# Windowed attention and a GELU feed-forward on one core: batch 1's denominators by pairs of pairs, its value products late, batch 0's tail queries loaded earlier

## Chip, cores and metric

The kernel runs on one core of a Trainium2 chip. The metric is the device time of one execution in microseconds (us). The core has five engines with instruction queues of their own: TensorE (PE; its weight loads are listed as PEld), VectorE (DVE), ScalarE (ACT), GpSimd (POOL) and SyncE (SP, which here only issues transfers). Each engine works through its queue in order. In the profile "PEq", "SPq" and so on are the sequencers; L613 is line 613 of the kernel.

## What is computed

```
# q, k, v: (8 batches, 8 heads, 576 positions, 64); w_in: (512, 2048); w_out: (2048, 512); float32
scores = (q @ k^T) / 8,  allowed where |i - j| <= 32
attn   = softmax(scores) @ v
x      = attn as (8 * 576 tokens, 512)
h      = x @ w_in
out    = (0.5 * h * (1 + tanh(c * (h + 0.044715 h^3)))) @ w_out        # 4608 x 512, float32
```

## The kernel before

**Tiles and stages.** The 4608 tokens go through the feed-forward in nine tiles of 512 (`t` = 0 to 8); a batch has 576 tokens. Attention is worked on by batch and, in it, by pairs of heads: four groups `g` = 0 to 3 of a pair each, for the first 480 positions (512 in batch 0), and a fifth group, the tail, for the last 96 (64) positions of all pairs. A stage `t` has two parts: products with `w_in` and GELU (`ffn_in`, 64 matmuls of 512 columns), then products with `w_out`. The second part of stage `t` is a loop over steps `i`, one output matmul each (`ffn_out_0`: 64 of 512 columns in stage 0; `ffn_out`: 112 of 256 columns from stage 1 on, a seven-product scheme `WINO` over halves of the matrices whose sums and differences DVE forms, L548 and L558). Between the steps batch `t + 1`'s attention is interleaved, and the tail of batch `t`. So stage 0's loop holds batch 1's attention and batch 0's tail, stage 1's loop holds batch 2's and batch 1's tail.

**The plan.** What comes before step `i` is written by hand in the dictionaries `PLAN_0` (stage 0), `PLAN_1` (stage 1) and `PLAN` (later): a letter, a group (-1 is the tail of the batch before), and after `@` which of two PSUM tiles (`S0`, `S1`, two banks each) is used.
- `s`: scores on PE and Exp on ACT (L410, L422). `m`: the mask, a DVE product with `band` (L428).
- `v`: `weigh` and `invert`: the sums (`ones` times the masked exps, L433), the products with values (L443), then the reciprocal of the sums on ACT as exp(-ln(sum)): L468 Ln, L469 Exp. Without `@` its two banks are `O` and `D`.
- `x`: `spread`, the DVE product of value products and reciprocals into `xT` (L478; L484 for a tail). It frees the banks.
- Stage 0 alone: `r` casts and transposes a pair of batch 1's queries and keys (L282 casts, L310 and L312 transposes, L317 and L318 copies out); `t` transposes batch 0's tail queries (L299, copied out by DVE in L303); `w`, `u` cast a quarter of `w_out` (L213) on DVE, POOL and ACT; `d` is `pair_chunk`, the DVE copies (L193, L195) that put a chunk of batch 1's V beside the next one; `c` starts the sums of `w_out` (L548).

The bank of a tile is taken again only when what was in it has been read: `v2@1` of stage 0 waits for `x0`, since both use `S1`.

**Transfers.** SP issues the loads of weights, queries and keys in program order. `tails_0` loads batch 0's last 64 queries (L154) and keys (L156) into a tile `tr`; `tails` loads batch 1's into the same buffer, so that SP waits there until `cast_tails` (L294) has read batch 0's. In the kernel before POOL does that cast of the queries at step 26, with `w2`. Then SP issues the last quarter of `w_out` (`wo[3]`) and, with `u3`, batch 2's queries and keys (`load_qk`, L168 to L173). Batch 1's V is loaded by POOL (`load_v`, L178, casting on the way; `load_vt`, L182). Batch 2's q and k are cast by DVE after stage 0 (L338, L362) and transposed by DMA (L341, L364); behind these SP loads batch 2's V (L370), which POOL casts (`cast_v`, L289) and DVE pairs (`pair_v`, L187 and L188) at steps 17 and 40 of stage 1, four heads each (`PAIR_1`). At step 4 of a stage POOL waits for the last key transpose (`after`, L819) and loads the next batch's V.

**DVE, stage 1.** The output products' seven results are taken out of PSUM by DVE when their 16 steps are done: M1 after step 15 (L624), U2 after 31 (L626), C11 after 47 (L628), U3 after 63 (L633), C22 after 79 (L636), C21 after 95 (L642).

Of the kernel before, what the change touches and what calls it, by code (L numbers as in the profile page):

```python
# [9 lines left out]
FP32 = mybir.dt.float32  # L10
# [26 lines left out]
def cut(b):  # L37
# [11 lines left out]

PLAN_0 = {8: "r2@0", 10: "s0@1", 11: "w1", 14: "s1@0", 19: "r3@1", 22: "m0 s2@0", 25: "s3@1", 26: "m1 w2",
          30: "t-1@0 m2", 35: "s-1@0 m3", 38: "d0", 39: "m-1", 40: "d1", 43: "v-1@0", 44: "d2 x-1 d3", 46: "w3",
          48: "v0@1 v1@0", 50: "x0 x1", 54: "v2@1", 55: "u3", 58: "v3@0 x2", 59: "x3", 60: "c1"}
PLAN_1 = PLAN | {10: "s0@0", 12: "s1@1", 18: "m0 m1", 33: "s2@0", 40: "v0@1 v1", 50: "x0", 53: "x1", 62: "s3@0 v2",
                 64: "s-1@1", 66: "m3", 70: "m-1", 76: "x2", 78: "v-1@1", 84: "x-1", 88: "s4@1", 91: "v3", 98: "m4"}
for i in (4, 16, 44, 80):
    del PLAN_1[i]
PAIR_1 = {17: slice(0, 4), 40: slice(4, 8)}

# [9 lines left out]
def kernel(  # L70
# [129 lines left out]
    def stage_w():  # L200
        return stage.tile([128, 4, 512], FP32, name="wst", tag="stage")
# [394 lines left out]
    def ffn_out(t, i):  # L596

        n, blk, f = i // 16, i // 8 % 2, i % 8
        a, w, new = WINO[n]
        end = t == NT - 1  # L600
        if i % 16 == 0 and new:
            pys[n % 2] = bank((1 + n) % 2)
            if end and n == 4:
                pys["apart"] = psO.tile([128, 512], FP32, name="py2", tag="O")
        py = pys[n % 2].rearrange("p (b c) -> p b c", b=2)
        apart = end and blk and n in (4, 6)
        if a[0] == "A":
            r0, c0 = 8 * (int(a[2]) - 1) + f, 256 * (int(a[1]) - 1) + 128 * blk
            lhsT = gTs[t][:, r0, c0:c0 + 128]
        else:  # L610
            lhsT = wino[a][:, f, 128 * blk:128 * blk + 128]
        one = end and n in (4, 6)
        nc.tensor.matmul(pys["apart"][:, 0:256] if apart else py[:, blk, :], lhsT,  # L613
                         wino[w][:, f, :], start=(new and i % (8 if one else 16) == 0),
                         stop=(i % (8 if one else 16) == (7 if one else 15)),
                         skip_group_check=True)
        if i % 16 < 15:
            return
        yo, left, right = wino["yo"], slice(0, 256), slice(256, 512)
        C11, C12, C21, C22 = (yo[:, r:r + 2, c] for r in (0, 2) for c in (left, right))  # L620

        M1, U2, U3 = C21, C12, C22
        if n == 0:
            nc.vector.tensor_copy(M1, py)  # L624
        elif n == 1:
            nc.vector.tensor_tensor(U2, py, M1, op=ALU.add)  # L626
        elif n == 2:
            nc.vector.tensor_copy(C11, py)  # L628
            if end:
                for x in range(2):  # L630
                    store(t, x, yo[:, x, :], left, nc.sync)
        elif n == 3:
            nc.vector.tensor_tensor(U3, py, M1, op=ALU.add)  # L633
        elif n == 4:
            if not end:
                nc.vector.tensor_tensor(C22, py, U3, op=ALU.add)  # L636
            else:
                for x, part in enumerate((py[:, 0, :], pys["apart"][:, 0:256])):
                    nc.vector.tensor_tensor(C22[:, x, :], part, U3[:, x, :], op=ALU.add)
                    store(t, 2 + x, yo[:, 2 + x, :], right, nc.sync, nc.scalar)  # L640
        elif n == 5:
            nc.vector.tensor_tensor(C21, py, M1, op=ALU.add)  # L642
            for x in range(2):
                store(t, 2 + x, yo[:, 2 + x, :], *((left, nc.sync, nc.scalar) if end else ()))
# [98 lines left out]
    for n in range(4):  # L743
        ffn_in(0, n, 3, 4)
    cast_w(wi[2], w_in16[:, :, 1024:1536], (0, 2))
    wo.append(load_w_out(1, stage_w()))
    qk(6)
    wo.append(load_w_out(2, stage_w()))
    tails_0("q")
    tails()  # L750
    wo.append(load_w_out(3, stage_w(), 0, 2))
    load_w_out(3, wo[3], 2, 4)
# [24 lines left out]
    trans_pair(1, 1, psO.tile([128, 8, 128], FP16, name="pt", tag="O"))  # L777
    cast_early(1, 2, (nc.vector, nc.vector))
    load_v(1, (2, 3))

    def spare(i):
        pt = psS.tile([128, 2, 8, 128], FP16, name="pt", tag=f"S{i}")
        return pt[:, 0], pt[:, 1]


    begun = 0
    for t in range(NT):
        b = t + 1
        att = b < B
        if t:  # L790
            for fc in range(begun):
                ffn_in(t, fc, 3, 4, then=False)
            for fc in range(begun):
                gelu(t, fc)
            if att and b > 1:
                rest = cast_and_turn(b)
            for fc in range(begun, NF):
                ffn_in(t, fc)
                if t == 1 and fc in (3, 4, 5, 6):
                    cast_v(2, fc - 3)  # L800
                if t == 1 and 9 <= fc < 14:
                    rest(fc - 9)
                if t == 1 and fc == 8:
                    trans_tails(1, psO.tile([128, 8, 128], FP16, name="pt", tag="O"))
                if t > 1 and fc == 8 and att:
                    pair_v(b, nc.vector.tensor_copy)
        plan = PLAN_0 if not t else PLAN_1 if t == 1 else PLAN if att else {5: "v-1", 31: "x-1"} if t == B - 1 else {}

        def group(g):
            return (b, g) if g >= 0 else (b - 1, 4)  # L810

        if plan and t:
            load_table(exp_set)
        if t and b + 1 < B:
            load_qk(b + 1)
        ods = {}
        for i in range(113 if t else 65):
            if t and i == 4 and b + 1 < B:
                nc.gpsimd.tensor_copy(after, KLs[b % 2][:, 3, 0:1])  # L819
                load_v(b + 1)  # L820
            for act in plan.get(i, "").split():
                kind, at = act[0], int(act[act.index("@") + 1:]) if "@" in act else None
                g = int(act[1:].split("@")[0])
                if kind == "w":
                    if g == 3:
                        cast_w(wo[g], w_out16[:, 12:16, :], cs=(0, 1), on_dve=(0,))
                    else:
                        cast_w(wo[g], w_out16[:, 4 * g:4 * g + 4, :], on_act=(1, 3))
                    if g == 1:
                        load_vt(1)  # L830
                    if g == 2:
                        cast_tails(0, nc.gpsimd, even)
                elif kind == "t":
                    trans_tails(0, spare(at)[0], even)
                elif kind == "r":
                    if g == 3:
                        cast_early(1, 3, (nc.vector, nc.vector))
                    trans_pair(1, g, *spare(at), copy=nc.scalar.copy)
                elif kind == "u":
                    cast_w(wo[g], w_out16[:, 12:16, :], on_dve=(3,), cs=(2, 3))  # L840
                    cast_tails(1, nc.gpsimd)
                    load_qk(2)
                elif kind == "c":
                    if g == 1:
                        B12 = combine_w()
                    combine(g, nc.vector)
                elif kind == "s":
                    score(*group(g), at)
                elif kind == "d":
                    pair_chunk(b, g, nc.vector.tensor_copy)  # L850
                elif kind == "m":
                    mask(*group(g))
                elif kind == "v":
                    bb, gg = group(g)
                    o, d = weigh(bb, gg, at)
                    ods[g] = (o, invert(bb, gg, d))
                    if t and g < 0 and b + 1 < B:
                        load_vt(b + 1)
                    if t and g == (3 if att else -1):
                        load_table(gelu_set)  # L860
                else:
                    spread(*group(g), *ods[g])
            if t == 1 and i == 30:
                cast_vt(2)
            if t == 1 and i in PAIR_1:
                pair_v(2, nc.vector.tensor_copy, PAIR_1[i])
            if t == 0 and i in (61, 62):
                store(0, *later.pop(0), slice(0, 512), nc.scalar)
            if t == 0 and i < 64:
                ffn_out_0(*ORDER_0[i])  # L870
            elif t and i < 112:
                ffn_out(t, i)
        if t == 0:
            for t4, yo in later:
                store(0, t4, yo)
            wino_rest(B12)
            load_table(gelu_set)
        else:
            ffn_last(t)
        begun = 3 if t < NT - 1 else 0  # L880
        for fc in range(begun):
            ffn_in(t + 1, fc, 0, 3)
# [28 lines left out]
```

## Time and profile before

| | |
|---|---|
| median of 6 runs | 304.02 us (303.69 to 305.15) |
| profiled execution | 304.11 us, its span 302.4 us |
| granted TensorE clock, mean | 0.992 |
| PE busy | 289.1 us, 96% of the span |
| DVE busy | 194.1 us, 64% |
| ACT busy | 194.1 us, 64% |
| POOL busy | 92.3 us, 31% |

The span runs from the first to the last instruction of the program. All times in the text are counted from its start. A busy PE is one whose matmuls are in flight; holes in it are found by engine and cause in the view of waits ("who waited: by whom released: us in total, times, longest"). The chain is the run of work that ended last, followed backwards. Stage 0's output part runs from 36.7 to 58.3 us, stage 1's first part to 72.4 and its output part to 92.8; each later stage takes about 30.4 us.

### The profile page before, as it was taken

To read this page: it belongs to the slowest core of one execution; us is meant where nothing else is said; L and a number is where in the kernel's file an instruction comes from. 1 tells how busy PE (TensorE), PEld (TensorE's weight loads), DVE (VectorE), ACT (ScalarE), POOL (GpSimd) and SP (SyncE) were. 2 spreads that over 40 slices of the span, in tenths; PEclk is the share of its full clock that TensorE was granted. 3 is DMA by queue.
4 is the path that set the end of the run, shared out by engine and by line. 5 is a ranking of instruction groups with operands and counts; after the bars stand their busy time and mean duration, and the time that the engine had idled before them with its cause. 6 is when DMAs were issued, how large, how long until landed. Compare 5 with 4: busy or idle time off the path is not lost.

```text
span 302.4 us, 7116 instructions
## 1 busy us (share of the span) xinstructions
PE 289.1 (96%) x2898; PEld 180.3 (60%) x2898; DVE 194.1 (64%) x435; ACT 194.1 (64%) x306; POOL 92.3 (31%) x142
## 2 busy tenths in 40 slices
PE   6879999999879999999999999999999999999994
PEld 2434454445755478547864786478647864784583
DVE  4537456697768866876687668766876635533452
ACT  5774684889566785678566866686668657705600
POOL 3445731111816060605071416050610050015000
PEclk9979999999999999999999999999999999999999
DMA  7999998999799989698979798989596031004013
GB/s 222 244 340 379 358 245 197 290 224 201 186 197 168 152 227 178 136 155 211 172 158 154 193 171 171 163 208 178 96 167 65 3 81 60 2 0 140 2 35 104
DMA packets 116550, 50.14 MB, mean 166 GB/s; under 512 B 97911, under 2 KB 109943, under 8 KB 116518
## 3 DMA queue, kind: packets, MB, share of 16 engines
q1 hardware_dynamic: 82644, 36.70, 58.6%
q0 software_dynamic: 32464, 11.42, 28.2%
q10 hardware_dynamic: 1410, 1.58, 1.6%
q8 instruction: 22, 0.36, 0.5%
q14 instruction: 10, 0.08, 0.1%
HBM read 36.70 MB, written 9.44 MB: 153 GB/s over the span
## 4 chain that ended last, share of the span: by engine, by line
PE 80%; DVE 7%; DMA 5%; SPq 2%; ACT 2%; issue 1%; POOL 0%; DVEq 0%
PE mm L613 29%; PE mm L515 19%; PE ph L515 17%; PE ps_s L410 3%; DMA vr<-in_v_dram 2%; PE ps_d L433 2%; PE ps_o L443 2%; DMA qr<-in_v_dram 2%; PE py L587 2%; PE mm L587 2%; DMA kr<-in_k_dram 1%; DVE t L548 1%; SPq L146 1%; ACT lt L468 1%; DVE xT L478 1%
## 5 line engine op out<-in xcount | busy, mean ns | idle before, releaser
L515 PEld LDWEIGHTS <-w_in 128*128 128x128 f16 x576 | 56.2, 98 | 66.4 <-issue 0.7
L515 PE MATMUL mm<-xT,w_in 128*128 128x512 f16 x304 | 74.7, 379 | 0.0
L523 ACT ACTIVATE gT<-mm 128x512 f16<-128x512 f32 x76 | 45.2, 597 | 39.0 <-PE mm L515 38.3
L515 PE MATMUL ph<-xT,w_in 128*128 128x512 f16 x272 | 68.2, 379 | 0.1
L577 POOL DMA_DIRECT2D out_dram<-y x55 | 32.8, 606 | 87.5 <-DVE y L642 78.6
L613 PEld LDWEIGHTS <-s 128*128 128x128 f16 x512 | 49.4, 98 | 6.0
L558 DVE TENSOR_TENSOR s<-gT 128x512 f16<-128x512 f16 x64 | 26.9, 420 | 36.2 <-ACT gT L523 36.2
L523 ACT ACTIVATE gT<-ph 128x512 f16<-128x512 f32 x68 | 37.9, 599 | 15.1 <-PE ph L515 15.1
L613 PE MATMUL mm<-t,s 128*128 128x256 f16 x376 | 45.1, 273 | 0.0
L613 PEld LDWEIGHTS <-gT 128*128 128x128 f16 x384 | 35.8, 98 | 6.7
L422 ACT ACTIVATE pe<-ps_s 128x960 f16<-128x960 f32 (+1 forms) x32 | 30.6, 976 | 13.3 <-PE ps_s L410 13.1
L613 PE MATMUL mm<-w_out,gT 128*128 128x256 f16 x256 | 33.2, 273 | 0.0
L469 ACT ACTIVATE lt<-lt 128x480 f32<-128x480 f32 (+3 forms) x40 | 23.5, 587 | 1.3
L95 ACT ACT_TABLE_LOAD x17 | 21.8, 1283 | 2.2 <-issue 1.9
L178 POOL DMA_DIRECT2D V<-in_v_dram x24 | 21.6, 917 | 1.9 <-issue 1.5
L468 ACT ACTIVATE lt<-ps_d 128x480 f32<-128x480 f32 (+2 forms) x28 | 15.5, 555 | 8.7 <-PE ps_d L433 5.6
L443 PEld LDWEIGHTS <-V 128*64 128x64 f16 x520 | 14.8, 114 | 7.9 <-DVE V L195 2.3
L428 DVE TENSOR_TENSOR pe<-pe,band 128x960 f16<-128x960 f16 x28 | 17.5, 650 | 1.0 <-ACT pe L422 1.0
L613 PE MATMUL mm<-t,gT 128*128 128x256 f16 x128 | 16.5, 273 | 0.0
L819 POOL COPY after<-KL 128x1 f16<-128x1 f16 x5 | 2.5, 510 | 42.9 <-DMA KL<-kt 42.9
L613 PE MATMUL mm<-w_out,s 128*128 128x256 f16 x120 | 14.4, 273 | 0.0
L410 PE MATMUL ps_s<-QT,KT 64*64 64x128 f16 (+3 forms) x576 | 13.8, 216 | 0.6 <-DVE KT L318 0.6
(104 smaller groups left out, 330.7 us busy)
## 6 DMA issues: line engine op xcount, KB each, us to landing
kr<-in_k_dram SPq DMA_DIRECT2D x31, 256.0 KB, 11.1
qr<-in_q_dram SPq DMA_DIRECT2D x6, 1024.0 KB
wst<-in_moe_w_in_dram SPq DMA_DIRECT2D x8, 512.0 KB, 8.4
wst<-in_moe_w_out_dram SPq DMA_DIRECT2D x3, 1024.0 KB, 12.7
V<-in_v_dram POOLq DMA_DIRECT2D x24, 128.0 KB, 9.1
qr<-in_q_dram SPq DMA_DIRECT2D x7, 256.0 KB, 9.0
out_dram<-y POOLq DMA_DIRECT2D x6, 192.0 KB, 6.1
vr<-in_v_dram SPq DMA_DIRECT2D x4, 256.0 KB, 7.1
```

Source lines behind the costliest of these rows:

```text
L95: nc.scalar.add_instruction(mybir.InstLoadActFuncSet(name=nc.get_next_instruction_name(), act_func_set_id=which, ins=[], outs=[]))
L178: nc.gpsimd.dma_start(V[:, c, :, :], v[b, :, 128 * c:128 * c + 128, :].rearrange("h p d -> p h d"))
L410: nc.tensor.matmul(ps[64 * half:64 * half + 64, h, 4 * n * r:4 * n * r + 4 * n].rearrange("k (j p) -> k j p", j=4)[:, :, p0 - q0:p1 - q0], ...
L422: nc.scalar.activation(pe, ps[:, :, 0:w], AF.Exp, scale=SCALE)
L443: nc.tensor.matmul(o[64 * h:64 * h + 64, cols].rearrange("d (j p) -> d j p", j=4)[:, :, p0 - q0:p1 - q0], Vs[b % 2][:, slot, 2 * pr + h, : ...
L468: nc.scalar.activation(lt[:, 0:n], d[:, 0:n], AF.Ln)
L469: nc.scalar.activation(lt[:, 0:n], lt[:, 0:n], AF.Exp, scale=-1.0)
L515: nc.tensor.matmul(ph, w_in16[:, dc, fc * 128:fc * 128 + 128], xT[:, dc, t * 512 % RING:t * 512 % RING + 512], start=(dc == 0), stop=(dc = ...
L523: nc.scalar.activation(gTs[t][:, fc, :], phs[fc], AF.Gelu_apprx_tanh)
L558: nc.vector.tensor_tensor(dst, x, y, op=op)
L577: eng.dma_start(out_v[b, j, q0 + p:q0 + p + e, cols], yo[m:m + e, cols])
L613: nc.tensor.matmul(pys["apart"][:, 0:256] if apart else py[:, blk, :], lhsT, wino[w][:, f, :], start=(new and i % (8 if one else 16) == 0) ...
```

## The change

In stage 0 the four groups of batch 1 are no longer worked one by one with `v`. Two new letters take two groups at once: `n` makes the sums of two pairs into the two banks of one `S` tile and has ACT take both logarithms and then both exponentials, into a new tile `lt4`; `p` makes both pairs' value products into one `S` tile. `n0` is at step 33 and `n2` at 38, `p0` at 50 and `p2` at 54; the `x` follow them. `lt4` takes one of the five `stage` buffers, and the tiles after it move on by one.

Batch 0's tail queries (`tails_0("q")`) are issued on SP ahead of `wo[1]`, batch 1's last pair (`qk(6)`) and `wo[2]`, no longer behind these. Their cast on POOL comes before the loop, no longer at step 26; their transposes are at step 18 (30), the tail's scores at 29 (35), its `v` at 44 (43), its `x` at 47 (44). `r3` goes from 19 to 21, `w2` from 26 to 30, `m2` and `m3` to 31 and 32, `d3` from 44 to 47.

In stage 1 the masks `m0 m1` go from step 18 to 16, ahead of the pairing at 17; the tail's scores, mask, products and spread go from 64, 70, 78, 84 to 58, 64, 74, 80, the next tail's scores `s4` from 88 to 86. C11 is copied by ACT in that stage, and batch 3's V is loaded at step 46 instead of 4.

```diff
-PLAN_0 = {8: "r2@0", 10: "s0@1", 11: "w1", 14: "s1@0", 19: "r3@1", 22: "m0 s2@0", 25: "s3@1", 26: "m1 w2",
-          30: "t-1@0 m2", 35: "s-1@0 m3", 38: "d0", 39: "m-1", 40: "d1", 43: "v-1@0", 44: "d2 x-1 d3", 46: "w3",
-          48: "v0@1 v1@0", 50: "x0 x1", 54: "v2@1", 55: "u3", 58: "v3@0 x2", 59: "x3", 60: "c1"}
-PLAN_1 = PLAN | {10: "s0@0", 12: "s1@1", 18: "m0 m1", 33: "s2@0", 40: "v0@1 v1", 50: "x0", 53: "x1", 62: "s3@0 v2",
-                 64: "s-1@1", 66: "m3", 70: "m-1", 76: "x2", 78: "v-1@1", 84: "x-1", 88: "s4@1", 91: "v3", 98: "m4"}
-for i in (4, 16, 44, 80):
+PLAN_0 = {8: "r2@0", 10: "s0@1", 11: "w1", 14: "s1@0", 18: "t-1@1", 21: "r3@1", 22: "m0 s2@0", 25: "s3@1", 26: "m1",
+          29: "s-1@0", 30: "w2", 31: "m2", 32: "m3", 33: "n0@1", 36: "m-1", 38: "n2@0 d0", 40: "d1", 44: "v-1@1 d2",
+          46: "w3", 47: "d3 x-1", 50: "p0@0 x0 x1", 54: "u3 p2@1", 55: "x2 x3", 60: "c1"}
+PLAN_1 = PLAN | {10: "s0@0", 12: "s1@1", 33: "s2@0", 40: "v0@1 v1", 50: "x0", 53: "x1", 58: "s-1@1", 62: "s3@0 v2",
+                 64: "m-1", 66: "m3", 74: "v-1@1", 76: "x2", 80: "x-1", 86: "s4@1", 91: "v3", 98: "m4"}
+PLAN_1[16] = "m0 m1"
+for i in (4, 44, 84):
     del PLAN_1[i]
...
-            nc.vector.tensor_copy(C11, py)
+            (nc.vector.tensor_copy if t > 1 else nc.scalar.copy)(C11, py)
...
     cast_w(wi[2], w_in16[:, :, 1024:1536], (0, 2))
+    tails_0("q")
     wo.append(load_w_out(1, stage_w()))
     qk(6)
     wo.append(load_w_out(2, stage_w()))
-    tails_0("q")
     tails()
...
     load_v(1, (2, 3))
-
+    cast_tails(0, nc.gpsimd, even)
...
+    lt4 = stage.tile([128, 4, 512], FP32, name="lt4", tag="stage")
...
-            if t and i == 4 and b + 1 < B:
+            if t and i == (4 if t > 1 else 46) and b + 1 < B:
                 nc.gpsimd.tensor_copy(after, KLs[b % 2][:, 3, 0:1])
                 load_v(b + 1)
...
-                    if g == 2:
-                        cast_tails(0, nc.gpsimd, even)
...
+                elif kind in "np":
+                    pair = psS.tile([128, 2, 512], FP32, name="ps_od", tag=f"S{at}")
+                    for x in range(2):
+                        if kind == "n":
+                            sum_up(1, g + x, pair[:, x, :], groups[(1, g + x)])
+                        else:
+                            ods[g + x] = (pair[:, x, :], lts[g + x])
+                            times(1, g + x, pair[:, x, :], groups.pop((1, g + x)))
+                    if kind == "n":
+                        n = size(1, g)
+                        lts[g], lts[g + 1] = lt4[:, g, :], lt4[:, g + 1, :]
+                        for x in range(2):
+                            nc.scalar.activation(lts[g + x][:, 0:n], pair[:, x, 0:n], AF.Ln)
+                        for x in range(2):
+                            nc.scalar.activation(lts[g + x][:, 0:n], lts[g + x][:, 0:n], AF.Exp, scale=-1.0)
```

## Prediction

> **What bounds the kernel now.** I read the busy time by stage first: stage 0's output part, stage 1's output part, and the same part of stage 2, which an undisturbed batch runs through.
>
> ```profile
> 36.60:58.30 21.70, 20.70 (x244) 9.91 (x242) 13.34 (x30) 15.58 (x26) 6.42 (x9) 1.00 1.21 245
> 72.40:92.80 20.40, 18.12 (x283) 13.92 (x282) 14.34 (x28) 14.38 (x21) 9.64 (x12) 1.00 1.20 187
> 106.60:123.20 16.60, 16.60 (x267) 13.72 (x266) 11.27 (x20) 12.79 (x18) 5.09 (x7) 1.00 1.28 183
> ```
>
> Columns: window, length, then busy time (count) of PE, PEld, DVE, ACT, POOL, granted clock, DMA share, GB/s. From stage 2 on PE has no hole. Stage 1 takes 3.8 us longer with one tail score more (0.34 us). So only the window 36 to 93 can give time back. Second view, PE's waits in it (the same view from 93 on is empty):
>
> ```profile
> PE ps_o L443 <- DVE xT L478: 1.0, 1, 1.0
> PE ps_od L433 <- DVE pe L428: 0.8, 1, 0.8
> PE ps_s L410 <- DVE xT L484: 0.5, 1, 0.5
> PE py L587 <- DVE KT L318: 0.5, 1, 0.5
> PE ps_od L443 <- DVE V L195: 0.3, 1, 0.3
> PE ps_od L433 <- DVE xT L478: 0.2, 1, 0.2
> ```
>
> Every one is a DVE result that is late. Third, the chain in that window says why DVE is late in stage 1:
>
> ```profile
> 71.74 5.14 DMA qr<-in_v_dram
> ...
> 76.94 0.62 POOL V L289
> ...
> 78.03 0.42 DVE V L188
> 78.44 1.13 DVE pe L428 x2
> ...
> 80.77 0.85 DVE V L187
> 81.63 0.86 DVE V L188
> 82.49 0.59 DVE y L628
> 83.08 1.27 DVE xT L478 x4
> ```
>
> Batch 2's values land at 76.9, POOL casts them, DVE pairs them, and only behind that come two masks that were ready earlier. Last, SP's own waits and the DMA queues in 36 to 42 and 42 to 46:
>
> ```profile
> SPq L154 <- DMA tr<-in_q_dram: 10.7, 1, 10.7
> ```
>
> ```profile
> q1 hardware_dynamic: 1252, 1.67, 90.3%
> q0 software_dynamic: 1145, 0.14, 36.6%
> ```
>
> ```profile
> q0 software_dynamic: 3180, 0.40, 156.6%
> q1 hardware_dynamic: 440, 0.21, 27.2%
> ```
>
> SP stands from 35.0 to 45.7 because batch 1's tails need the tile that batch 0's tail queries still fill. Meanwhile its queue (q1) runs dry and POOL's queue (q0: batch 1's values) takes the engines.
>
> **Stage 0 (36.7 to 58.3).** 64 output matmuls at a 0.2165 us pitch make 13.9; everything else on PE about 5.3; the rest is holes. Three stand in the tail, read from PE's timeline: 52.04 to 52.46 (copy of V chunk 3), 54.38 to 54.70 (v2's bank, held until x0), 56.13 to 56.44 (behind the cast of w_out chunk 15 on DVE, itself queued behind x1): 1.05. In the change the sums and the Ln/Exp of all four pairs come at steps 33 and 38, so x0 to x3 wait for products alone. The sums are the same matmuls; Ln, Ln, Exp, Exp is the same four activations, dependent ones no longer adjacent (Ln and Exp now start 0.6 apart, independent activations of this width about 0.5). ACT: scores' exps, two casts, eight activations and the tail's two reach about 53.4 by their rows, where ACT now idles 1.57 and 1.42 before 50.5 and 52.75. The tail's spread x-1 is then done at 53.8, and p2 needs its bank only at 54.6: covered by 0.8; if ACT slips further, p2 slips one for one.
>
> Added: t-1 at step 18 puts its query copy (L303) ahead of the last q and k casts on DVE. These start 40.4 and 41.1 now; they would start about 43.2 and 43.55, and r3 on PE wants them at 43.1 and 43.6: a stall of 0.35 (0 to 0.6). A new switch between sums and products adds 0.1, and I keep 0.1 for the masks being due at once at step 38. The tail queries pass four transfers on SP: two of w_out, a q and a k. Their 512 short packets cost these about 1.0 us (the tails of 47 to 49 show 621 packets in one us): wo[1] 38.9 to 39.9, the k piece 41.0 to 42.0, wo[2] 44.4 to 45.4. First uses are 42.1, 43.6 and (step 32) 47.8, so nothing, which ends if the delay is over 2 us. On POOL the tail cast (0.61) goes before w1's cast and one V issue: hidden, w1's third chunk is wanted at step 28. Net: 1.05 - 0.55 = **0.5 saved** (0.9 saved to 0.4 lost).
>
> SP is free at about 38.9 instead of 46.4. So q1 no longer runs dry, and batch 1's V must share. V's chunk 3 ends with packet 4096; 1145 are through by 42, 2950 remain. At the ratio of 36 to 42 (1145 to 1252) that needs 3230 packets of q1: the rest of wo[2] (about 180), two tails (1024), wo[3] (512), q (1024), 490 of k; at some 190 (2 KB), 300 (1 KB) and 450 (256 B) per us it is there at 52.4 instead of 47.5. Its pairing (d3, 0.6) ends at 53.0; p0 wants it at 53.05. I take no cost, with no margin.
>
> DVE after that: x3 ends 56.8 instead of 59.0; with a copy between, batch 2's q casts start about 59.2 instead of 60.65, so SP's transposes, the V loads and POOL's casts behind them come 1.45 sooner (0 to 1.9): last V cast 76.1 instead of 77.55. q and k of batch 2 have landed by then, since SP issues them about 7 us earlier.
>
> **Stage 1.** Masks m0 m1 move ahead of the pairing: now 78.22 to 79.06 PE waits 0.84 for them; in the change they end at 76.7, the pairing at 77.5, and v0 comes at 77.6: saves 0.75. Second hole, 83.24 to 84.39 (1.15, v2's bank, held until x1): x0 and x1 stand on DVE behind U2, m2, the second pairing and C11's copy. U2 and m2 start about 1.5 to 2 sooner, and C11 (0.66) goes to ACT, between v1's Exp (80.3) and the tail score's exp (81.2): a hidden 0.57. x0 ends about 80.7 and the tail score, moved to step 58, wants its bank at 80.7: 0.1 remains (0 to 0.5). Saves 1.05. Third, 88.55 to 89.25 (0.70, s4 until x-1): s-1, m-1, v-1, x-1 and s4 all move up, s4 still finds x-1 about 0.6 late, and v-1 now waits about 0.3 for m-1 behind U3: 0.2 lost. Sum **1.5 to 1.6; I take 1.5** (0.5 to 2.2).
>
> The load of batch 3's V moves from step 4 to 46. POOL's order then is vt's cast, the wait for the last transpose, four issues of 0.91: about 79.7 to 83.3, as now. It is still beside the second pairing, which shows 0.85 and 0.86 there against 0.42 and 0.42 alone; that is in the sum. [...]
>
> **Stage 2.** Its first scores run at 107.18; their key transposes land at 106.12 by the trace's semaphores, a margin of 1.06. PE comes 2.0 sooner; the transposes follow casts of queries that move with PE, but key casts that wait for a load (95.54) that moves 1.45. I take 0.2 lost (0 to 0.9).
>
> **Sum.** 0.5 + 1.5 - 0.2 = 1.8. The profiled execution took 304.11 (span 302.4 and 1.71 around it), 0.09 over the median of 304.02. Span 300.6, execution 302.3, median **302.2 us**.
>
> **Rivals.**
> Slower: batch 1's V chunk 3 comes too late. Its pairing holds x-1, x0, x1 and the cast of w_out chunk 15 on DVE, and p0 on PE. Each us past 53 costs one. In the us from 36 to 37 V got only 141 packets for q1's 246; at that ratio it would land near 56.7. With 56, stage 0 loses 3.0 - 0.5 = 2.5, stage 1 still saves 1.0: 305.5. It decides the sign from about 54.5 to 55 on. For it: the change frees SP into just this time. Against: the 6 us of nearly equal turns. Chance 0.11.
> Capped: the key transposes of stage 2, or batch 2's V, don't move, so only the margin of 1.06 is won: 303.0. For it: SP issues transposes and loads in one row from 62.1 to 78. Chance 0.20 (302.8 to 303.4).
> No change: the tail queries still land as late (SP's place is not what delays them) and stage 0 loses what stage 1 wins: 304.0. Chance 0.08.
> More: all three holes of stage 1 go and r3 doesn't stall: 300.9. Chance 0.05.
> Forecast, 301.4 to 302.8: 0.56.
>
> The measurement tells a difference of 0.2% (0.6 us) from none. Faster is forecast, capped and more: 0.81; same 0.08; slower 0.11. The range 301.0 to 303.8 leaves out the slow case, a part of no change, and the low end.
>
> **What would show it.** SP's wait at L154 near nothing and batch 1's tails issued about 39; V chunk 3 landing before 53; FFN matmuls of stage 1 starting about 57.8 (58.3 now) and of stage 2 near 90.8 (92.8); PE's waits without L428 and without the 1.0 at L443. Wrong if PE waits on L193/L195 for over 1 us, if r3 waits over 0.6, or if PE waits at stage 2's first scores.

## The result: 1.009 times the time before

| | before | changed |
|---|---|---|
| median, us (lowest to highest) | 304.03 (302.65 to 306.01), 41 runs | 307.01 (304.73 to 309.64), 20 runs |
| profiled execution (span), us | 304.11 (302.4) | 305.73 (304.0) |
| stage 0's output part starts, us | 36.68 | 34.60 |
| stage 1 starts, us | 58.30 | 61.78 |
| stage 1, length, us | 34.53 | 32.58 |
| stage 2, length, us | 30.42 | 30.41 |

The ratio is 1.009 (95% interval 1.0071 to 1.011): slower, where 302.2 was forecast. The ratios here and below leave disturbed executions out; the medians are of all. Here the profiled execution is one of the quicker ones; it places the loss, and the runs size it. Stage 1 starts 3.48 us later and is 1.95 us shorter: 1.53 of the 1.59 us by which the spans differ. Stage 0's output part began 2.08 us sooner here, so it is 5.56 us longer in all. The half of the forecast on stage 1 came true in direction, and the half on stage 0 was turned over.

PE's waits from 36 to 95, in the changed kernel (who waited, by whom released: us in total, times, longest):

```profile
PE ps_od L445 <- DVE V L197: 2.5, 1, 2.5
PE mm L589 <- DVE w_out L215: 1.8, 2, 1.4
PE ps_s L412 <- DVE xT L486: 0.6, 1, 0.6
PE ps_od L435 <- DVE pet L430: 0.2, 1, 0.2
```

The waits of before for masks (0.8) and for the spread (1.0) are gone. Two new ones are larger: `p0` waits 2.5 us for the pairing of batch 1's values, and an output matmul 1.4 us for a quarter of `w_out`. The chain from 30 to 60 says what the first goes back to:

```profile
36.32 0.82 POOL V L180
37.13 18.53 DMA V<-in_v_dram
...
55.69 0.04 DVE V L195
...
55.99 0.29 DVE V L197
...
56.33 0.72 PE ps_od L445 x10
```

V's chunk 3, issued at 37.13, has landed in full only at 55.67; in the kernel before it was there at 47.49, 10.2 us after its issue. DVE's timeline shows that the second wait has the same root:

```profile
51.43 0.56 DVE L195 COPY V<-V 64x512 f16<-64x512 f16 x1 [2.99 <-DMA V<-in_v_dram]
52.01 0.60 DVE L197 COPY V<-V 64x512 f16<-64x512 f16 x1
52.54 0.41 DVE L215 CAST w_out<-wst 128x512 f16<-128x512 f32 x1
55.69 0.29 DVE L195 COPY V<-V 64x512 f16<-64x512 f16 x1 [2.75 <-DMA V<-in_v_dram]
55.99 0.28 DVE L197 COPY V<-V 64x512 f16<-64x512 f16 x1
56.20 0.41 DVE L486 TENSOR_TENSOR xT<-ps_od,lt 128x256 f16<-128x256 f32 x1
```

DVE stands 2.99 us for chunk 2 (`d2`, landed 51.41; 46.66 before). The cast of `w_out` is behind `d2` in DVE's queue, although its data landed at 49.51 and 51.19. The wait "on the cast of w_out" is a wait on V. `x-1` is in turn behind `d3`. And PE, in this stretch:

```profile
53.00 0.59 PE L589 MATMUL mm<-w_out,gT 128*128 128x512 f16 x2 [1.36 <-DVE w_out L215]
53.52 0.36 PE L445 MATMUL ps_od<-pe,V 128*64 128x96 f16 x10
56.33 0.72 PE L445 MATMUL ps_od<-pe,V 128*64 128x64 f16 x18 [2.46 <-DVE V L197]
56.98 1.03 PE L589 MATMUL py<-w_out,gT 128*128 128x512 f16 x2
57.81 1.06 PE L589 MATMUL mm<-w_out,gT 128*128 128x512 f16 x2
...
60.91 0.59 PE L589 MATMUL mm<-w_out,gT 128*128 128x512 f16 x2
```

Two matmuls of 512 columns, 0.59 before and afterwards, take 1.03 and 1.06 after the long wait. The window from 57 to 58 gives the reason (columns as in the prediction; granted clock third from last):

```profile
57.00:58.00 1.00, 1.00 (x5) 0.41 (x4) 0.91 (x2) 0.00 (x0) 0.00 (x0) 0.50 0.57 127
```

The clock is 0.50 for 3.41 us, 55.94 to 59.36: by an estimate from these two numbers at most 1.7 us more. The page of the changed kernel has it as the 7 in the eighth slice:

```profile
PEclk9999999799999999999999999999999999999998
```

Where V lost its time shows in the DMA queues, from 42 to 46 (queue, kind: packets, MB, share of 16 engines). Before, POOL's queue q0 sent 3180 packets in this window and SP's q1 440:

```profile
q0 software_dynamic: 2030, 0.26, 98.6%
q1 hardware_dynamic: 1121, 0.51, 66.5%
```

SP is the one that brings q1 in. Its waits for the tails' buffer from 18 to 66 in the changed kernel, 4.3 us together, where the kernel before stood 10.7 us:

```profile
SPq L156 <- DMA tr<-in_q_dram: 2.6, 1, 2.6
SPq L156 <- POOL t L296: 1.7, 1, 1.7
```

Batch 1's tails are issued at 38.66, no longer at 46.36, and behind them the last quarter of `w_out` and batch 2's queries. The landing time is that of the prediction's slower rival, 56.

### The profile page after: what moved, and what is told of

The parts are those of the page before. It is cut to its first block, busy times and chain, and to the rows that moved or that the text cites. A ratio compares the mean times of both kernels' runs of the same rounds, so it can differ in the third digit from the quotient of the medians.

```text
span 304.0 us, 7118 instructions
## 1 busy us (share of the span) xinstructions
PE 289.8 (95%) x2898; PEld 179.9 (59%) x2898; DVE 192.7 (63%) x434; ACT 193.8 (64%) x307; POOL 92.8 (31%) x142
## 3 DMA queue, kind: packets, MB, share of 16 engines
q10 hardware_dynamic: 1410, 1.58, 1.6%
## 4 chain that ended last, share of the span: by engine, by line
PE 79%; DMA 14%; SPq 3%; DVE 1%; POOL 1%; issue 0%; ACT 0%
PE mm L615 32%; PE mm L517 20%; PE ph L517 16%; DMA V<-in_v_dram 6%; DMA wst<-in_moe_w_out_dram 3%; PE ps_s L412 3%; DMA wst<-in_moe_w_in_dram 3%; PE ps_d L435 2%; PE ps_o L445 2%; SPq L148 2%; DMA tr<-in_k_dram 2%; SPq L206 1%; PE ps_od L445 1%; PE py L589 1%; PE ps_od L435 1%; POOL w_out L215 1%
## 5 line engine op out<-in xcount | busy, mean ns | idle before, releaser
L579 POOL DMA_DIRECT2D out_dram<-y x55 | 32.9, 607 | 86.3 <-DVE y L644 77.7
L525 ACT ACTIVATE gT<-ph 128x512 f16<-128x512 f32 x68 | 37.9, 599 | 13.5 <-PE ph L517 13.5
L471 ACT ACTIVATE lt<-lt 128x480 f32<-128x480 f32 (+3 forms) x36 | 21.1, 585 | 1.1
L430 DVE TENSOR_TENSOR pe<-pe,band 128x960 f16<-128x960 f16 x28 | 18.2, 670 | 1.0 <-ACT pe L424 1.0
## 6 DMA issues: line engine op xcount, KB each, us to landing
kr<-in_k_dram SPq DMA_DIRECT2D x31, 256.0 KB, 10.5
```

The source lines that it names most:

```text
L430: nc.vector.tensor_tensor(pe, pe, m.rearrange("k (o j) p -> k o j p", o=1).broadcast_to(list(pe.shape)), op=ALU.mult)
L471: nc.scalar.activation(lt[:, 0:n], lt[:, 0:n], AF.Exp, scale=-1.0)
L525: nc.scalar.activation(gTs[t][:, fc, :], phs[fc], AF.Gelu_apprx_tanh)
L579: eng.dma_start(out_v[b, j, q0 + p:q0 + p + e, cols], yo[m:m + e, cols])
```

## Experiments

The theory after the result: the sooner release of SP is the loss, stage 1's changes are a gain, and `n`/`p` matter little. Rivals: `n`/`p` themselves cost the time; the 512 short packets of the tail queries do; or the order of SP's transfers does. Every kernel is compared with the kernel before, on the same chip. The stage lengths are of one profiled execution each; "half" is a stretch of half clock in stage 0's tail. Stage 0's length goes with its start too: of the kernels without a half clock there, those that start it by 35.4 take 22.9 to 24.1 us for it, and those that start it from 36.2 on 21.5 to 22.1; so its start stands before its length. Their sum is stage 1's start: 57.4 to 59.9 in every kernel without a half clock there, 61.8 to 65.2 in the four with one. Of e12_wo3_free only the time is used.

| kernel | stage 0: start, length | stage 1 | V chunk 3, issue to landing | half | median, us (before beside it) | ratio, 95% interval |
|---|---|---|---|---|---|---|
| before | 36.68, 21.62 | 34.53 | 10.2 | no | 304.03 | |
| changed | 34.60, 27.18 | 32.58 | 18.5 | yes | 307.01 | 1.009, 1.0071 to 1.011 |
| e1_stage1 | 37.95, 21.62 | 33.35 | 10.5 | no | 303.03 (303.98) | 0.9967, 0.9942 to 0.9993 |
| e2_tails | 36.71, 28.47 | 34.28 | 18.8 | yes | 309.14 (303.98) | 1.0163, 1.0128 to 1.0198 |
| e4_hold | 37.63, 22.10 | 35.57 | 15.9 | no | 307.86 (303.98) | 1.0118, 1.0071 to 1.0165 |
| e5_np | 38.04, 21.84 | 33.62 | 10.2 | no | 303.65 (303.98) | 0.9992, 0.9964 to 1.0021 |
| e6_np_stage1 | 34.28, 23.51 | 32.87 | 10.2 | no | 302.60 (303.90) | 0.9957, 0.993 to 0.9983 |
| e7_hold_all | 35.43, 26.51 | 32.65 | 10.5 | yes | 307.16 (303.90) | 1.01, 1.0065 to 1.0135 |
| e8_wo3_first | 36.97, 21.54 | 32.70 | 13.7 | no | 302.48 (303.90) | 0.9942, 0.9919 to 0.9966 |
| e9_load_only | 35.18, 24.11 | 33.95 | 10.5 | no | 305.00 (303.90) | 1.0033, 1.0007 to 1.0058 |
| e10_wo3_hold | 36.20, 21.96 | 36.99 | 13.5 | no | 306.92 (303.62) | 1.0106, 1.0077 to 1.0136 |
| e11_stage1_wo3 | 34.47, 22.93 | 33.20 | 14.0 | no | 302.32 (303.62) | 0.9945, 0.9915 to 0.9976 |
| e12_wo3_free | | | | | 307.31 (303.62) | 1.0101, 1.0067 to 1.0134 |
| e13_s4_late | 35.39, 23.23 | 32.04 | 13.9 | no | 301.52 (303.62) | 0.9916, 0.9889 to 0.9942 |
| e14_hold0 | 34.67, 23.94 | 32.74 | 11.5 | no | 305.12 (304.19) | 0.9989, 0.9951 to 1.0027 |
| e15_wo3_hold0 | 36.81, 22.13 | 33.18 | 16.9 | no | 308.20 (304.19) | open |
| e16_load | 34.23, 24.04 | 32.72 | 10.5 | no | 304.00 (304.19) | 1.0001, 0.9965 to 1.0036 |
| e17_load_cast | 35.71, 27.33 | 32.58 | 18.9 | yes | 307.95 (304.19) | 1.0137, 1.0091 to 1.0184 |

### The parts one by one

**Stage 1 alone.** The kernel before with the new `PLAN_1`, C11 copied by ACT, and the load of batch 3's V at step 46.

```diff
...
-for i in (4, 16, 44, 80):
+PLAN_1[16] = "m0 m1"
+for i in (4, 44, 84):
...
+            (nc.vector.tensor_copy if t > 1 else nc.scalar.copy)(C11, py)
...
+            if t and i == (4 if t > 1 else 46) and b + 1 < B:
```

> The kernel before with only the change's stage 1 part (its PLAN_1, C11 on ACT, batch 3's V at step 46); stage 0 and all transfers before it are the old ones. Transfer theory (the whole loss comes from SP's transfers that run sooner and hold up batch 1's V): stage 1's saving stands by itself, its part from first FFN matmul to stage 2's first takes 32.6 to 33.2 instead of 34.5, the run 302.0 to 303.0. Plan theory (late products in stage 0 are the loss): the same here. Third: stage 1 was only short in the changed kernel because batch 2's data had longer to arrive behind a slow stage 0; then PE waits for the pairing of V at step 40 and the run takes 303.4 to 304.2.

Measured: 303.03 us, 0.9967, at the upper end of what was expected. Stage 1 takes 1.18 us less, and stage 0 is the same to the hundredth. The gain of this half is real, and the interval leaves out no change only just. Its size is less sure than the stage length makes it look, since stage 1 also starts 1.27 us later here (see e5_np).

**The sooner tail queries alone**, load and cast.

```diff
     cast_w(wi[2], w_in16[:, :, 1024:1536], (0, 2))
+    tails_0("q")
     wo.append(load_w_out(1, stage_w()))
     qk(6)
     wo.append(load_w_out(2, stage_w()))
-    tails_0("q")
     tails()
...
+    cast_tails(0, nc.gpsimd, even)
...
-                    if g == 2:
-                        cast_tails(0, nc.gpsimd, even)
```

> The kernel before with only batch 0's tail queries loaded and cast sooner, as in the change; plans as before. Transfer theory: SP is free at about 39, batch 1's V chunks 2 and 3 land near 51 and 55 instead of 46.7 and 47.5, DVE stands at d2 and d3 (planned 3 steps earlier than in the change), PE waits 3 to 6 us for them: 306 to 309. Plan theory: the transfers alone cost nothing, w_out's last quarter comes sooner: 303.5 to 304.2.

Measured: 309.14 us, 1.0163, slower than the whole change and a little over the range expected. PE's first wait from 36 to 100:

```profile
PE ps_od L443 <- DVE V L195: 4.6, 2, 3.4
```

V's chunk 3 needs 18.8 us here, with neither `n` nor `p` in the kernel. The loss is in the transfers.

**The change with SP held.** A load of 128 bytes out of V's chunk 3 stands ahead of `load_qk(2)`, so that SP waits there for the chunk.

```diff
+    hold = const.tile([1, 64], FP16, name="hold")
...
+                    nc.sync.dma_start(hold, Vs[1][0:1, 3, 0, :])
                     load_qk(2)
```

> The changed kernel with one small transfer added on SP ahead of batch 2's queries and keys; it reads batch 1's V chunk 3, so SP goes on only when that has landed. Tails and w_out's last quarter still run sooner. Transfer theory: with batch 2's 2.25 MB out of the way chunk 3 lands at 50 to 52 instead of 55.7, PE's wait for its pairing falls from 2.5 to under 0.7, no half clock follows, and stage 1's saving shows: 301.5 to 303.3. Plan theory: PE still waits over 1.5 in the tail of stage 0: 305 to 307.

Measured: 307.86 us, 1.0118, and the expectation missed. Stage 0 takes 22.10, from a late start (37.63) and with no half clock. V's chunk 3 still lands at 53.99, with the tails and `w_out` still going ahead of it. But batch 2's queries and keys now come late, and stage 1 takes 35.57, with many small waits where the changed kernel had two (0.6 and 0.2):

```profile
...
PE ps_od L446 <- DVE V L191: 0.6, 1, 0.6
PE ph L518 <- ACT gT L526: 0.4, 1, 0.4
PE mm L518 <- ACT gT L526: 0.4, 1, 0.4
PE mm L616 <- DVE y L627: 0.4, 1, 0.4
```

**`n` and `p` alone**, with the old transfers and the old stage 1.

```diff
-          30: "t-1@0 m2", 35: "s-1@0 m3", 38: "d0", 39: "m-1", 40: "d1", 43: "v-1@0", 44: "d2 x-1 d3", 46: "w3",
-          48: "v0@1 v1@0", 50: "x0 x1", 54: "v2@1", 55: "u3", 58: "v3@0 x2", 59: "x3", 60: "c1"}
+          30: "t-1@0 m2", 33: "m3 n0@1", 35: "s-1@0", 38: "d0", 39: "m-1", 40: "d1", 42: "n2@0", 44: "v-1@1 d2 d3",
+          46: "w3", 47: "x-1", 50: "p0@0 x0 x1", 54: "u3 p2@1", 55: "x2 x3", 60: "c1"}
...
```

> The kernel before with only the sums of two pairs at once (n at 33 and 42) and the late products (p at 50 and 54), tails transposed, loaded and cast as before, stage 1 as before. Transfer theory: V lands at 47.5 as before, so the late products find it; PE may wait about 0.6 for w_out's last quarter (lands at 52.3): 303.3 to 304.6. Plan theory: the tail of stage 0 stalls as in the change, 306 or more.

Measured: 303.65 us, 0.9992, an interval on both sides of one. Stage 0 takes 21.84 against 21.62: the three holes in its tail, summed at 1.05 in the prediction, give no time back. It isn't a loss either, so the first rival falls. Stage 1, which this kernel leaves as it was, takes 33.62, 0.91 less than before: it starts 1.58 later, and PE's wait of 0.8 for masks is not there. So part of any shorter stage 1 behind a later start is the start, not the plan.

### Which transfer must not share

**`n`/`p` and stage 1 together, the transfers as before** (the edits of e1_stage1 and e5_np in one kernel).

```diff
...
+          30: "t-1@0 m2", 33: "m3 n0@1", 35: "s-1@0", 38: "d0", 39: "m-1", 40: "d1", 42: "n2@0", 44: "v-1@1 d2 d3",
...
+PLAN_1[16] = "m0 m1"
+for i in (4, 44, 84):
...
```

> The kernel before with sums and products of two pairs (n at 33 and 42, p at 50 and 54) and the stage 1 part; all transfers as before. Transfer theory: everything of the change but the sooner tail queries is good or neutral; stage 0 takes 21.6 to 22.2, stage 1 32.4 to 33.4 (34.5 before), the run 301.5 to 303.0. Rival (the parts work only apart: p and the earlier stage 1 fall onto each other): no better than the stage 1 part alone, 303.0 or more.

Measured: 302.60 us, 0.9957. The change without the sooner tail queries, and with the steps of `PLAN_0` that go with them where they were, is faster than before. In the profiles it starts stage 0's output part nearly where the changed kernel does (34.28; 34.60) and is through it 3.99 us sooner.

**The change with everything behind the tail queries held** until V's chunk 3 is there.

```diff
...
     wo.append(load_w_out(2, stage_w()))
-    tails()
-    wo.append(load_w_out(3, stage_w(), 0, 2))
-    load_w_out(3, wo[3], 2, 4)
...
     cast_tails(0, nc.gpsimd, even)
+    nc.sync.dma_start(hold, Vs[1][0:1, 3, 0, :])
+    tails()
+    wo.append(load_w_out(3, stage_w(), 0, 2))
+    load_w_out(3, wo[3], 2, 4)
```

> The changed kernel, but SP holds batch 1's tails, w_out's last quarter and all behind them until batch 1's V chunk 3 has landed (a small transfer that reads it). The tail queries themselves still load and are cast sooner. Transfer theory: V lands 10 to 12 us after its issue as before, against 18.5; w_out's last quarter at 53 to 55 makes PE wait 0.5 to 1.5; stage 1 saves over 1: 302.0 to 304.0. If the sooner tail queries or the changed plan were the cause by themselves, V or the products are still late: 305.5 or more.

Measured: 307.16 us, 1.01, a miss. V's chunk 3 is back at 10.5 us, as before. Now `w_out`'s last quarter is the late one (54.85 and 56.23), and PE waits 3.3 us for it, where it waited 2.5 for V:

```profile
PE mm L590 <- DVE w_out L216: 3.3, 1, 3.3
```

There is little spare time here: V, the tails, the last quarter and batch 2's queries all have their due times close together, and what was held back here to help V was missed itself.

**The last quarter of `w_out` ahead of the tails**, on e6_np_stage1.

```diff
     wo.append(load_w_out(2, stage_w()))
     tails_0("q")
-    tails()
     wo.append(load_w_out(3, stage_w(), 0, 2))
     load_w_out(3, wo[3], 2, 4)
+    tails()
```

> As the run with n, p and the stage 1 part on the old transfers, but SP issues w_out's last quarter ahead of batch 1's tails, so ahead of its wait. That is 512 packets of 2 KB beside V's. Transfer theory: V chunk 3 lands 2 to 4 us later than without (about 50 to 52), still before p0 wants it; PE's wait for w_out's last quarter goes: 301.3 to 302.8. Rival (any traffic of SP there stretches V past its use): V past 53 and 303.5 or more.

Measured: 302.48 us, 0.9942. It shares with V, which lands at 51.07, 13.7 us after its issue, and that is still in time: the longest wait in stage 0's tail is 0.2. The interval overlaps that of e6_np_stage1, so the order by itself is not shown to gain.

**The tail queries loaded sooner but cast at step 26 still.**

```diff
     cast_w(wi[2], w_in16[:, :, 1024:1536], (0, 2))
+    tails_0("q")
     wo.append(load_w_out(1, stage_w()))
     qk(6)
     wo.append(load_w_out(2, stage_w()))
-    tails_0("q")
```

> The kernel before with the tail queries issued sooner on SP, but cast by POOL where it was (with w2), so that SP is freed no sooner. Only the place of that cast differs from the run that had load and cast sooner (309.1). Transfer theory: SP still waits until about 46, V lands near 47.5 to 49: 303.7 to 304.8. If the 512 short packets ahead of w_out are the cause by themselves: 306 or more.

Measured: 305.00 us, 1.0033. So 512 short packets ahead of `w_out` cost 1.1 us by the medians, 0.2 to 1.8 by the interval, while V lands as before. That lies between the two ranges expected. In the profile from 36 to 100 the new waits are small: 0.5 for a query cast, 0.4 for a key cast, 0.5 for `w_out`, 0.8 for the tail cast. The last is 1.2 in e6_np_stage1, which loads the tail queries as before, so it does not belong to the load.

### Other orders

**`w_out`'s last quarter first, the rest held for V's chunk 3**, on the change.

```diff
...
-    tails()
     wo.append(load_w_out(3, stage_w(), 0, 2))
     load_w_out(3, wo[3], 2, 4)
...
     cast_tails(0, nc.gpsimd, even)
+    nc.sync.dma_start(hold, Vs[1][0:1, 3, 0, :])
+    tails()
```

> The changed kernel with w_out's last quarter issued ahead of batch 1's tails, and tails and batch 2's queries and keys held until batch 1's V chunk 3 has landed. So what stage 0 wants by 52 (V, w_out) goes first, what is wanted later goes last; the sooner tail queries and the whole plan of the change stay. Order theory (the loss is that transfers wanted later share the DMA engines with the two wanted first): V chunk 3 lands at 50 to 53, w_out's last quarter by 50, PE waits for the two together under 1.0 us; 302.3 to 304.0. Rival (the changed plan of stage 0 cannot hide even that; or the sooner tail queries cost what they cost in any order): 305 or more.

Measured: 306.92 us, 1.0106, a miss. Stage 0 is as short as before (21.96), and stage 1 is the longest of all, 36.99. DVE's waits from 56 to 80:

```profile
DVE k L365 <- DMA kr<-in_k_dram: 4.5, 1, 4.5
DVE q L341 <- DMA qr<-in_q_dram: 1.8, 1, 1.8
```

Batch 2's first queries land at 61.39, no longer at 56.76. The hold only handed the delay on.

**Stage 1 and the order of `w_out`, without `n`/`p`** (the edits of e1_stage1 and e8_wo3_first).

```diff
...
-for i in (4, 16, 44, 80):
+PLAN_1[16] = "m0 m1"
+for i in (4, 44, 84):
...
-    tails()
     wo.append(load_w_out(3, stage_w(), 0, 2))
     load_w_out(3, wo[3], 2, 4)
+    tails()
```

> The kernel before with the stage 1 part and w_out's last quarter ahead of batch 1's tails on SP; sums and products of stage 0 as before, pair by pair. Order theory: V chunk 3 lands near 51 as in the run with n and p (it landed there at 51.1 against 46.8), but here d3 stands at step 44 and v0 at 48, so DVE and PE wait 0.5 to 1.5 us: 302.8 to 304.0, worse than with n and p (302.5). Rival (n and p win nothing by themselves): 302.3 to 302.7.

Measured: 302.32 us, 0.9945, the same as with `n`/`p` (0.9942), and so the rival's time: these gain nothing in the time. In single profiles with nothing held, stage 1 is some 0.5 us shorter with them (32.6 to 32.9, against 33.20 and 33.35 without); no comparison of times shows it.

**The same order on the change, nothing held.**

```diff
-    tails()
     wo.append(load_w_out(3, stage_w(), 0, 2))
     load_w_out(3, wo[3], 2, 4)
+    tails()
```

> As the run before it, but without the hold: w_out's last quarter first, then tails and batch 2's queries and keys as soon as SP is free. Order theory: these still share with V's last 2000 packets, V chunk 3 lands at 53 to 56 and PE waits 1 to 2.5 us for its pairing, but not for w_out: 304.0 to 306.5, between the changed kernel and the run with the hold. Rival (only w_out's lateness counted): as the run with the hold.

Measured: 307.31 us, 1.0101, over the range expected. The order doesn't mend what the sooner release does.

**The next tail's scores later**, on e8_wo3_first.

```diff
-                 64: "m-1", 66: "m3", 74: "v-1@1", 76: "x2", 80: "x-1", 86: "s4@1", 91: "v3", 98: "m4"}
+                 64: "m-1", 66: "m3", 74: "v-1@1", 76: "x2", 80: "x-1", 91: "s4@1 v3", 98: "m4"}
```

> The best version so far (n, p, stage 1 part, w_out's last quarter ahead of the tails, old tail queries) with stage 1's second tail scores at step 91 instead of 86, ahead of v3. PE's wait of 0.59 for x-1 there is covered by five output matmuls (0.54): stage 1 32.1 to 32.3 instead of 32.7, the run 301.8 to 302.3. If the mask behind these scores or x3 becomes late instead: 302.5 or more.

Measured: 301.52 us, 0.9916 (0.9889 to 0.9942). This version beats both kernels, by a little more than expected. `s4`'s wait of 0.6 for `x-1` is gone from PE's waits from 36 to 100, and stage 1 is the shortest of all, 32.04:

```profile
PE pt L300 <- POOL t L295: 1.3, 1, 1.3
PE pt L313 <- DVE k L283: 0.5, 1, 0.5
PE ps_od L434 <- ACT pet L423: 0.2, 1, 0.2
PE mm L588 <- DVE w_out L214: 0.2, 1, 0.2
PE ps_od L434 <- DVE pet L429: 0.2, 1, 0.2
```

Its interval overlaps that of e8_wo3_first. That it is faster than before is shown, that the 0.6 us come in full is not.

### Held for less, and the cast by itself

**Held only for V's chunk 0**, everything (e14_hold0) or all but `w_out`'s last quarter (e15_wo3_hold0): as e7_hold_all and e10_wo3_hold, with

```diff
+    nc.sync.dma_start(hold, Vs[1][0:1, 0, 0, :])
```

> The changed kernel with SP held, ahead of batch 1's tails, until batch 1's V chunk 0 has landed (43.7 to 45 in the runs so far), so that it goes on about when the old wait ended (46). Release theory: V chunk 3 lands near 50, w_out's last quarter at 51 to 53, batch 2's queries as before; PE waits under 1.5 us for the two together, stage 1 saves its 1.5 to 2: 302.5 to 304.8. Rival (not the release but the sooner tail queries with the changed plan): 306 to 308 as with the other holds.

> The changed kernel with w_out's last quarter ahead of that hold on V chunk 0. Release theory: as the best order of the old tail queries (302.5) plus up to 1.1 us for the 512 short packets ahead of w_out (the run that had them alone: 305.0 against 303.9): 302.3 to 304.0; stage 1 not over 33.5. Rival: 306 to 308.

Measured: 305.12 and 308.20 us, the first just over its range and the second in its rival's. With everything held for chunk 0, V needs 11.5 us, and the ratio (0.9989) can't be told from one, with a median 0.93 above that beside it; the longest wait in the tail is 1.6, for `w_out`. The other scatters from 302.29 to 311.53, far wider than the kernel before beside it (303.15 to 306.27). Four executions take 302.3 to 304.4, the profiled one (303.72) among them, with granted clocks of 0.992 to 1.000; the other eight take 307.3 or more, with clocks of 0.981 to 0.989. By the four alone the ratio would be 0.996 (0.9922 to 0.9999). Where the eight lose their clock no profile here shows, so this one stays open.

**The load and the cast apart.** e16_load is e6_np_stage1 with the load of the tail queries moved as in e9_load_only. e17_load_cast is e16_load with one POOL cast in another place:

```diff
     load_v(1, (2, 3))
+    cast_tails(0, nc.gpsimd, even)
...
-                    if g == 2:
-                        cast_tails(0, nc.gpsimd, even)
```

> The kernel with n, p and the stage 1 part (302.6) with the tail queries issued sooner on SP, still cast with w2 on POOL. Packets theory: the 512 short packets ahead of w_out and the last q and k cost what they cost alone (305.0 against 303.9), so 303.2 to 304.2; V lands as before, 10 to 11 us after its issue. Rival (the load costs nothing once the products are late): 302.2 to 302.9.

> The same with the cast sooner too, so that SP goes on at about 39. Release theory: V chunk 3 lands 17 to 19 us after its issue, PE waits 1.5 to 4 us for its pairing and the half clock follows: 306 to 309. Rival (the late products hide it; the changed kernel loses by where its plan puts the tail's steps): 303.0 to 304.5.

Measured: 304.00 us and 307.95 us, against 304.19. The load costs 1.1 (0.19 under the time before, where e6_np_stage1 was 1.30 under), as in e9_load_only; the intervals of the two, up to 0.9983 and from 0.9965, overlap a little. The place of the cast costs 3.95 more, with the same instructions and the same bytes. SP's waits from 18 to 66, e16_load first:

```profile
SPq L155 <- POOL t L295: 9.8, 1, 9.8
```

```profile
SPq L155 <- POOL t L295: 1.5, 1, 1.5
```

The DMA queues from 42 to 46, again e16_load first:

```profile
q0 software_dynamic: 3392, 0.43, 168.6%
q1 hardware_dynamic: 121, 0.22, 16.7%
```

```profile
q0 software_dynamic: 1697, 0.21, 81.9%
q1 hardware_dynamic: 1149, 0.60, 73.1%
```

While SP stands 9.8 us, q0 sends 3392 packets in this window to q1's 121; freed after 1.5 us, it brings q1 to 1149, and q0 is halved to 1697. In e17_load_cast PE's wait names `w_out`:

```profile
PE mm L588 <- DVE w_out L214: 4.0, 1, 4.0
```

and DVE's timeline from 51 to 58 names V:

```profile
55.75 0.29 DVE L194 COPY V<-V 64x512 f16<-64x512 f16 x1 [3.09 <-DMA V<-in_v_dram]
56.05 0.28 DVE L196 COPY V<-V 64x512 f16<-64x512 f16 x1
56.26 0.41 DVE L214 CAST w_out<-wst 128x512 f16<-128x512 f32 x1
```

That settles the cause: the sooner cast, through SP's release. e7_hold_all is the other half of the proof: with the same sooner cast, but SP held, V's chunk 3 needed 10.5 us.

## Why the prediction was wrong, step by step

- **The step that failed: "it is there at 52.4 instead of 47.5 ... I take no cost, with no margin."** V's chunk 3 was there at 55.67. The direction was right and SP's release was foreseen to the quarter us (38.9; 38.66). The sum was one of packets over all 16 engines. By that count V was even ahead of the forecast: q0 sent 1014, 2030 and 1424 packets from 36 to 42, to 46 and to 52, 4468 in all, where the sum wanted 4096 by 52.4. But of the sixteen landing updates of this chunk, the first ten came from 47.41 to 48.12 and the last two at 55.23 and 55.67, and the copy that waited for it started at 55.69, behind the last: the sum had no term for that. In the kernel before all sixteen came from 45.03 to 47.49, so that there the mean and the last looked alike. Why some updates lag so far no run here shows; the spread of 8.3 us is what no mean could give.
- **The price of being late.** "Each us past 53 costs one" gave 305.5 for a landing at 56, with a chance of 0.11. What a late chunk holds up was right. The landing time was right by luck: its reason was that V would get 141 packets for q1's 246, but from 42 to 46 V got 2030 for q1's 1121, and it was the last landing updates that were late. The price lacked at least two terms: chunk 2, late as well (51.41) and ahead of `w3`'s cast on DVE (1.36 on PE), and the half clock from 55.94 to 59.36, which begins within `p0`'s wait (at most 1.7 by the estimate above). The 1.0 us that this price left to stage 1 no run shows; the stage was 1.95 us shorter. The kernel took 307.01.
- **"The tail queries pass four transfers ... so nothing."** Measured by itself twice, 1.1 us (e9_load_only; e16_load against e6_np_stage1, less surely). The single uses were compared with their due times, and each seemed to have room; the profiles show several waits of about 0.5 us and no one place for the sum.
- **Stage 0, "0.5 saved".** `n` and `p` alone save nothing there (21.84 for 21.62). In e5_np PE waits 0.5 for `w_out` and 0.2 for the tail's exponentials in their place. The 1.05 was also read too large: in the three holes PE's timeline marks waits of 0.33, 0.15 and none. The stall of 0.35 for `r3` that was set against it is not among the changed kernel's waits.
- **Stage 1, "I take 1.5" (0.5 to 2.2): inside the range, the size not settled.** The stage is 1.95 shorter in the changed kernel and 1.18 alone, where it starts 3.48 and 1.27 later; in e5_np a start 1.58 later gave 0.91 with the old plan. By the medians the stage 1 part alone gains 0.95. The wait for masks, which went in e5_np too, and the wait for the spread, which stayed there (1.1), are gone, and `s4` finds `x-1` 0.6 late as forecast. C11's copy on ACT is not seen to delay PE.
- **The pairing beside POOL's loads**, from DVE's timeline of the changed kernel:

```profile
82.76 0.42 DVE L189 COPY V<-V 64x1024 f16<-64x1024 f16 x1
83.20 0.69 DVE L190 COPY V<-V 64x768 f16<-64x768 f16 x1
```

The 0.42 and 0.69, with POOL's four issues running from 82.74 to 86.32, are less than the 0.85 and 0.86 that were in the sum. In e5_np one such copy took 1.16 (from 81.25, beside POOL's issues from 78.61 to 82.16), 0.74 over the 0.42. What sets the length of these copies no run here shows.

- **Stage 2, "0.2 lost": nothing lost** (30.41 for 30.42).
- **The range.** 301.0 to 303.8 left out the slower case whole. Between the pairing's end (53.0) and p0's due time (53.05) lay 0.05 us, on a landing forecast from a mean: that is too thin for a chance of 0.11.
- **What was to show it wrong** did: PE waits for L197 for over 1 us.

## What to carry to other kernels

A wait of an issuing engine can be what schedules the transfers (V's chunk 3 took 10.5 us where SP stood 9.8 us in e16_load, and 18.9 where it stood 1.5 in e17_load_cast): before removing it, list what it holds back, and who shares the DMA engines once it is let go. Forecast a load's landing by its last landing update, not by packets over the mean rate (here 55.67, with ten of the sixteen there by 48.12), and give a chance of a miss that fits a margin of zero. In a full stretch, holding one transfer back for another only moved the delay (e4_hold 307.86 us, e7_hold_all 307.16, e10_wo3_hold 306.92); and the instruction that a wait names may itself only have stood behind the one that was late in its engine's queue, as the cast of `w_out` (56.26) stood behind V's pairing (55.75) in e17_load_cast.

## What the runs showed of the hardware

- The clock was halved for 3.41 us in stage 0's tail in each profile used here with a PE wait of 2.46 us or more there (the changed kernel 2.46, e7_hold_all 3.3, e2_tails 3.4, e17_load_cast 4.0), and in none whose longest wait there was 1.6 or less. In the changed kernel a wait of 1.36 that ended at 53.00 stood ahead of the 2.46 that ended at 56.33. Where between 1.6 and 2.46 the difference begins, and whether the wait alone makes it, no run here shows.
- The first output part starts anywhere from 34.2 to 38.0 us, though up to there the kernels differ only in the order of a few transfers and one cast: near 17 us an execution has half clock for 0 (the changed kernel, start 34.60), 3.41 (the kernel before, 17.77 to 21.19, start 36.68) or 6.83 us (e1_stage1, e4_hold, e5_np, starts 37.63 to 38.04). Two profiles are therefore compared by stage and by where each stage starts, not by the span alone.
- One V chunk, which POOL's queue sends in packets of 128 bytes (2030 packets, 0.26 MB in the window above), needed 10.2 us from issue to landing in the kernel before, where SP's queue sent only 440 packets from 42 to 46, and 18.5 to 18.9 us beside SP's loads: in the changed kernel (1121 packets of SP's queue in that window), in e2_tails and in e17_load_cast (1149).
